# Top-k attention and a Smelu MLP: Smelu from one read of PSUM, the softmax division issued at a step's end, and the first MLP products of a chunk placed among the last ones of the chunk before

## The chip, the core and the metric

The kernel runs on one core of a Trainium2 chip. The metric is device time in microseconds of one execution. TensorE is called PE here, VectorE DVE, ScalarE ACT, GpSimd POOL, and SyncE SP, as the profile calls them.

## What is computed

Top-k attention over 8 batches, 8 heads, 576 positions and head size 64, and behind it an MLP whose activation is Smelu with beta 1:

```python
scores = (1 / np.sqrt(D)) * np.matmul(q, k.transpose(0, 1, 3, 2))
kth = np.partition(scores, -32, axis=-1)[..., -32:-31]
scores = np.where(scores >= kth, scores, -1000000000.0)
attn = np.exp(scores - np.max(scores, axis=-1, keepdims=True))
attn = attn / (np.sum(attn, axis=-1, keepdims=True) + 1e-09)
x = np.matmul(attn, v)                    # then (B, H, S, D) -> (B*S, H*D) = 4608 x 512
h = x @ w_in                              # 512 x 2048
g = np.where(h >= 1, h, np.where(h <= -1, 0.0, (h + 1) ** 2 / 4))
return g @ w_out                          # 2048 x 512
```

The weights of the MLP arrive as float64 and are turned into float32 in the kernel.

## The kernel before

**Steps.** Attention is cut into 144 steps. A step is one tile of 128 queries (or the 64 positions that are left over, two heads at a time) and one pair of heads; DVE does the search for the 32 largest of 576 scores in it (`weights`, lines 271 to 329): four rounds of `max` (L283) and `match_replace` (L292) on the pairwise maxima (L269, L297 makes the pairwise minima), then the masked sum (L312) of the exponentials that ACT wrote (L287), and the reciprocal `rz` (L318). POOL then scales the weights `e` by `rz` (L325; in the early steps PE does it through a diagonal matrix, L322 and L342) and notes a difference in `excess` (L327). `weights` is a generator; each `next` on it issues one part. The last part is the one from `rz` to `excess`.

The rest of a step's attention is on PE and ACT: scores (`scores`, L258, copied out of PSUM by L261), transposes of the weights (`transpose_w`, L344 and L352, copied by L345 and L353), and the product with the values (`values`, L364 and L372, copied into `xT` by L377 and L379). Keys and queries are transposed as they are needed (L214, L222, L238).

**The MLP.** Tiles of 128 tokens are gathered into chunks of one or two tiles (21 chunks; the first four are worked a tile at a time, so with 128 columns, the later ones with two tiles at once, 256 columns). A chunk has 16 units of first products: `hidden` (lines 391 to 415) makes four products into one PSUM tile `ph` (L394) and then Smelu. With `r = relu(h/2 + 1/2)` (L398) and `g = relu(h - 1)` (L412), both read from PSUM by ACT, POOL makes `min(r, 1)` (L413), its square (L414), and adds it to `g` (L415). `r` has 2 buffers, `g` has 16, one for each unit. While weights are still being converted, units with odd `f` square on ACT (L408). The last chunk works on DVE in place of POOL (L403 to L405). For each tile there are 8 units of output products: `final` (L422) makes two 512-column products into the PSUM tile `py`, which has one buffer; behind the last one ACT copies it to `y` (L426) and SP stores it. `ph` and the value product share three PSUM buffers; scores, transposes of the weights, and those of keys and queries share four.

**The order.** All engines but SP run in the program's order, which the planner at the end of `run` writes out (lines 605 to 657). Step `m` begins, when the weights are converted, with the value product of step `m-2` and the scores of step `m+2`; then come seven slots. Slot by slot, `parts` says how many parts of `weights` are issued, slot 2 has the transposes of step `m-1`, slot 4 the transposes of queries and keys, and `advance` issues MLP units from the queue `pending`, as far as the step's `share` lets it. `share` is the smaller of the remaining work over the remaining steps and the pending work over the steps until the next chunk is complete. What is left of `weights` after the slots is issued at the step's end. When a chunk's last value product has been issued, `values_until` appends its units to `pending`: first products, then output products.

```python
parts = [1] * SLOTS if early else [1, 2, 2, 2, 0, 0, 0]
```

With these numbers all seven parts are issued by slot 3, so POOL's queue has L325 and L327 ahead of the Smelu units of slots 3 to 6.

Of the kernel before, what the change touches and what calls it, by code (L numbers as in the profile page):

```python
# [10 lines left out]
F32 = mybir.dt.float32  # L11
U32 = mybir.dt.uint32
I32 = mybir.dt.int32
AF = mybir.ActivationFunctionType
ALU = mybir.AluOpType
# [8 lines left out]
def kernel(  # L24
# [10 lines left out]
    nc = tc.nc  # L35
    B, H, S, D = q.shape
    NTOK, DM = out.shape
    DFF = moe_w_in.shape[1]
    P = 128
# [10 lines left out]
    NF = DFF // P  # L50
# [4 lines left out]
    const = ctx.enter_context(tc.tile_pool(name="const", bufs=1))  # L55
    ident = const.tile([P, P], F32, name="ident")
    make_identity(nc, ident)
    half = const.tile([P, 1], F32, name="half")
    nc.gpsimd.memset(half, 0.5)
    minus = const.tile([P, 1], F32, name="minus")  # L60
    nc.gpsimd.memset(minus, -1.0)
    two = const.tile([P, 1], F32, name="two")
    nc.gpsimd.memset(two, 2.0)

# [17 lines left out]
    n_pieces = NK * DFF // WC + NF * DM // WC  # L82
# [64 lines left out]
    def run(ctx, paired):  # L147
# [240 lines left out]
        def mlp(xT, tiles, pool, last):  # L388
            gs, pys = {}, {}

            def hidden(f, c0, c1):
                ph = ps.tile([P, CW], F32, name="ph", tag="ph", bufs=3)[:, 0:c1 - c0]
                for kk in range(NK):
                    nc.tensor.matmul(ph, w_in[:, kk, f * P:(f + 1) * P], xT[:, kk, c0:c1],  # L394
                                     start=(kk == 0), stop=(kk == NK - 1))

                r = pool.tile([P, CW], F32, name="r", bufs=2)[:, 0:c1 - c0]
                nc.scalar.activation(r, ph, AF.Relu, bias=half, scale=0.5)  # L398
                if f not in gs:
                    gs[f] = pool.tile([P, CW], F32, name="g", bufs=NF)  # L400
                g = gs[f][:, c0:c1]
                if last:
                    nc.vector.tensor_scalar(g, ph, -1.0, 0.0, ALU.add, ALU.max)  # L403
                    nc.scalar.activation(r, r, AF.Square)
                    nc.vector.scalar_tensor_tensor(out=g, in0=r, scalar=1.0, in1=g, op0=ALU.min, op1=ALU.add)  # L405
                    return
                if converted < n_pieces and f % 2:
                    nc.scalar.activation(r, r, AF.Square)  # L408
                    nc.scalar.activation(g, ph, AF.Relu, bias=minus, scale=1.0)
                    nc.gpsimd.tensor_scalar(r, r, 1.0, 0.0, ALU.min, ALU.max)  # L410
                else:
                    nc.scalar.activation(g, ph, AF.Relu, bias=minus, scale=1.0)  # L412
                    nc.gpsimd.tensor_scalar(r, r, 1.0, 0.0, ALU.min, ALU.max)  # L413
                    nc.gpsimd.tensor_tensor(out=r, in0=r, in1=r, op=ALU.mult)  # L414
                nc.gpsimd.tensor_tensor(out=g, in0=r, in1=g, op=ALU.add)  # L415

            def final(i, f0, f1):
                if f0 == 0:
                    pys[i] = ps.tile([P, DM], F32, name="py", tag="py")
                py = pys[i]  # L420
                for f in range(f0, f1):
                    nc.tensor.matmul(py, gs[f][:, i * P:(i + 1) * P], w_out[:, f, :],  # L422
                                     start=(f == 0), stop=(f == NF - 1))
                if f1 == NF:
                    y = pool.tile([P, DM], F32, name="y", bufs=1)
                    nc.scalar.copy(y, py)  # L426
                    for p0, p1, rows in rows_of(*tiles[i]):
                        nc.sync.dma_start(out=rows, in_=y[p0:p1])

            def hiddens(i0, i1):  # L430
                return [(NK * (i1 - i0), NK * (f * P // WC + 1), gs, True, partial(hidden, f, i0 * P, i1 * P))
                        for f in range(NF)]

            def finals(i):
                return [(2 * DM // P, n_pieces - (NF - f - 2) * (DM // WC), gs, False, partial(final, i, f, f + 2))
                        for f in range(0, NF, 2)]

            return gs, hiddens, finals


        rounds, chunks = [], []
# [8 lines left out]
        steps = []  # L450
        for b, t in rounds:
            tile_of = (b, t) if t < NT else (b - b % 2, t)
            ch = next(n for n, tiles in enumerate(chunks) if tile_of in tiles)
# [3 lines left out]
        n = len(steps)  # L457

        EARLY_CHUNKS = 4
# [9 lines left out]
        pending = deque()  # L469
        total, spent = sum(len(tiles) for tiles in chunks) * (NK * NF + NF * DM // P), 0  # L470
        converted, inspected, due = 0, 0, 0.0
# [26 lines left out]
        K_TIME, PIECE_TIME, UNIT_TIME, SLOTS, EARLY_STEPS, EARLY_SHARE = 9.6, 0.55, 0.22, 7, 4, 20  # L498
# [88 lines left out]
        def values_until(m):  # L587
            nonlocal valued, pe_time
            while valued < min(m, n):
                pe_time = max(pe_time, transposed + 1.8) + 1.25  # L590
                values(state[valued])
                state[valued] = None
                if valued in ready:
                    ch, i0, i1 = ready[valued]
                    if i0 == 0:
                        mlps[ch] = mlp(xTs[ch], chunks[ch], mlp_pool, ch == len(chunks) - 1)
                    gs, hiddens, finals = mlps[ch]

                    rest = [work for work in pending if work[2] is gs and not work[3]]
                    while pending and pending[-1][2] is gs and not pending[-1][3]:  # L600
                        pending.pop()
                    pending.extend(hiddens(i0, i1) + rest + [work for i in range(i0, i1) for work in finals(i)])
                valued += 1

        for m in range(n + 2):
            early = converted < n_pieces
            coming = min((r + 2 - m for r in ready if r + 2 > m), default=1)
            if not early:
                values_until(m - 1)
                begin_at(m + 2)  # L610
            share = min((total - spent) / (n + 2 - m), sum(work[0] for work in pending) / coming)
            top_k, parts = None, [0] * SLOTS
            if m < n:
                top_k = weights(state[m], state[m + 1] if m + 1 < n else None)
                parts = [1] * SLOTS if early else [1, 2, 2, 2, 0, 0, 0]
                start = max(dve_time, scored[m])
                now_converting = range(SLOTS) if m < EARLY_STEPS else range(0, SLOTS, 2)
                dve_time = start + K_TIME + PIECE_TIME * min(len(now_converting), n_pieces - converted)
                done[m] = dve_time
                state[m]["by_tensor"] = early  # L620
            for slot in range(SLOTS):
                now = start + (dve_time - start) * (slot + 1) / SLOTS
                for _ in range(parts[slot]):
                    next(top_k, None)
                if m < n and converted < n_pieces:
                    if slot in now_converting:
                        convert(now)
                elif slot == 3:
                    inspect()
                if slot == 1 + (not early) and 1 <= m <= n:  # L630
                    pe_time = max(pe_time, done[m - 1] + 2.0) + 1.0
                    transpose_w(state[m - 1])
                    transposed = pe_time
                if slot == 2 and m == n and paired:
                    judge(ps, att)
                if slot == 2 and early:
                    values_until(m)
                if m == 0 and slot in (1, 2):
                    next(first)
                if slot == 4 and early:  # L640
                    begin_at(m + 2)
                if slot == (5 if early else 4):
                    queries(m + 3)
                    if m < n and prep is None and next_keys < B and steps[m][0] == next_keys - 1 and steps[m][1] >= 1:
                        prep = keys_of(next_keys)
                    if prep is not None and m % 2 == 0:
                        got = next(prep, None)
                        pe_time += 0.5
                        if got is None:
                            prep, next_keys = None, next_keys + 1  # L650
                        else:
                            keys[next_keys] = got
                advance(min(share, EARLY_SHARE if early else share) / SLOTS if m < n else 0.0, now, not early)
            for _ in (top_k if top_k is not None else ()):
                pass
# [50 lines left out]
```

## Time and profile before

| | us |
|---|---|
| median of 3 runs | 1746.18 (1745.42 to 1746.61) |
| the profiled execution | 1746.35 |
| its span, from the first to the last record | 1744.5 |
| PE busy in the span | 1639.4 (94%) |
| DVE busy | 1537.0 (88%) |
| ACT busy | 1083.2 (62%) |
| POOL busy | 946.9 (54%) |
| mean granted clock of PE | 0.982 |

The shares are means over the span. The page's second part shows them in 40 slices, and they differ: in the first tenth PE is busy five to eight tenths and DVE seven to nine; after that PE is at nine tenths or more in each slice but the last, DVE goes between eight and nine until the last two slices, and POOL between one and eight. Records of PE have modelled ends, so that a PE shown as busy may still have gaps.

The page's fourth part, the chain of work that ended last, puts 65% of the span to PE, 14% to DVE, 11% to POOL and 6% to ACT. In the fifth part a group is a line, an engine and a kind of operation, with its count, its busy time and the mean duration of one, and behind the bar the idle time ahead of it and what ended that. The waits are the same idle times summed by who waited for whom. An engine works its queue in order, so whatever stands behind a waiting instruction waits too. A product of float32 matrices is two records on PE.

### The profile page before, as it was taken

How to read it: one execution, taken by the hardware profiler on the slowest of the kernel's cores; microseconds unless marked ns; L12 is line 12 of the kernel's file. 1: busy time of each engine (PE TensorE's matmuls, PEld its weight loads, DVE VectorE, ACT ScalarE, POOL GpSimd, SP SyncE). 2: the span in 40 equal slices, each digit the busy share in tenths (PEclk: the TensorE clock that was granted, in tenths of full speed). 3: DMA queues.
4: the chain of work that ended last, by engine and by line, in shares of the span. 5: the costliest groups of instructions: out<-in, count | busy, mean ns of one | idle time of the engine just before them, and what ended most of it. 6: DMA issues, size and time to landing. Idle time of an engine off the chain costs nothing.

```text
span 1744.5 us, 33535 instructions
## 1 busy us (share of the span) xinstructions
PE 1639.4 (94%) x10665; PEld 1151.5 (66%) x10665; DVE 1537.0 (88%) x4875; ACT 1083.2 (62%) x2942; POOL 946.9 (54%) x1668
## 2 busy tenths in 40 slices
PE   5588989999999999999999999999999999999998
PEld 4476575667766757476756767567667666666665
DVE  7999979888899999999987999999997998899752
ACT  6688575676667857576655647556555555466452
POOL 5689183665544817264646645436365554555550
PEclk7799999999999999999999999999999999999999
DMA  8333112111121112111200101000010000000000
GB/s 253 116 98 97 46 30 65 44 43 41 42 63 52 44 49 65 46 49 41 62 13 22 25 22 44 17 24 17 23 39 19 19 10 14 13 7 7 7 7 15
DMA packets 116668, 74.63 MB, mean 43 GB/s; under 512 B 87296, under 2 KB 95488, under 8 KB 116480
## 3 DMA queue, kind: packets, MB, share of 16 engines
q1 hardware_dynamic: 116480, 72.37, 14.5%
q8 instruction: 87, 1.43, 0.3%
q14 instruction: 101, 0.83, 0.2%
HBM read 62.91 MB, written 9.44 MB: 41 GB/s over the span
## 4 chain that ended last, share of the span: by engine, by line
PE 65%; DVE 14%; POOL 11%; ACT 6%; issue 3%; DMA 0%; POOLq 0%; DVEq 0%; SPq 0%; ACTq 0%
PE py L422 25%; PE ph L394 18%; PE sp L258 7%; PE po L364 7%; PE pw L344 5%; DVE tops L283 4%; DVE more L292 3%; POOL g L415 3%; POOL r L414 3%; DVE e L312 3%; POOL e L325 2%; POOL r L413 2%; ACT s L261 1%; DVE seconds L300 1%; ACT r L398 1%
## 5 line engine op out<-in xcount | busy, mean ns | idle before, releaser
L394 PE MATMUL ph<-xT,w_in 128*128 128x128 f32 (+1 forms) x3200 | 558.0, 326 | 14.4 <-ACT g L412 13.2
L422 PE MATMUL py<-w_out,g 128*128 128x512 f32 x1152 | 530.9, 600 | 2.0 <-ACT y L426 2.0
L394 PEld LDWEIGHTS ph<-xT,w_in 128*128 128x128 f32 x3200 | 472.3, 192 | 87.9 <-ACT g L412 26.0
L325 POOL TENSOR_SCALAR e<-e,rz 128x576 f32<-128x576 f32 x264 | 195.0, 750 | 520.2 <-DVE rz L318 488.8
L283 DVE MAX8 tops<-more 128x8 f32<-128x288 f32 x1152 | 465.4, 445 | 0.0
L292 DVE MATCH_REPLACE8 more<-tops,more 128x288 f32<-128x288 f32 x864 | 375.6, 442 | 0.0
L422 PEld LDWEIGHTS py<-w_out,g 128*128 128x128 f32 x1152 | 205.2, 190 | 224.1 <-issue 215.8
L312 DVE SCALAR_TENSOR_TENSOR e<-s,kth,e 128x576 f32<-128x576 f32 x288 | 245.7, 881 | 116.6 <-ACT e L287 116.3
L398 ACT ACTIVATE r<-ph,half 128x128 f32<-128x128 f32 (+1 forms) x400 | 166.5, 416 | 216.8 <-POOL g L415 156.7
L415 POOL TENSOR_TENSOR g<-r,g 128x128 f32<-128x128 f32 (+1 forms) x384 | 255.9, 666 | 30.2
L413 POOL TENSOR_SCALAR r<-r 128x128 f32<-128x128 f32 (+1 forms) x368 | 173.2, 471 | 132.0 <-ACT r L398 131.7
L414 POOL TENSOR_TENSOR r<-r 128x128 f32<-128x128 f32 (+1 forms) x368 | 213.9, 581 | 30.7
L261 ACT ACTIVATE s<-sp 128x288 f32<-128x288 f32 x576 | 195.2, 421 | 56.8 <-PE sp L258 36.8
L287 ACT ACTIVATE e<-s,nmax 128x576 f32<-128x576 f32 x288 | 213.4, 770 | 7.7
L364 PEld LDWEIGHTS po<-wT,v_in 128*64 128x64 f32 x2048 | 111.8, 137 | 87.9 <-issue 53.2
L258 PE MATMUL sp<-kT,qT 64*128 64x288 f32 x1024 | 163.9, 437 | 4.2 <-ACT kT L218 2.3
L364 PE MATMUL po<-wT,v_in 128*64 128x128 f32 x2048 | 145.5, 280 | 18.7 <-ACT g L412 11.3
L345 ACT COPY wT<-pw 128x512 f32<-128x512 f32 x288 | 154.0, 589 | 13.1 <-PE pw L344 10.6
L344 PEld LDWEIGHTS pw<-ident,e 128*128 128x128 f32 x1056 | 122.2, 142 | 60.0 <-issue 24.4
L344 PE MATMUL pw<-ident,e 128*128 128x128 f32 x1056 | 141.0, 276 | 16.2 <-ACT s L261 10.4
L377 ACT COPY xT<-po 128x128 f32<-128x128 f32 x128 | 34.1, 266 | 195.8 <-PE po L364 195.5
L412 ACT ACTIVATE g<-ph,minus 128x128 f32<-128x128 f32 (+1 forms) x368 | 153.6, 417 | 0.0
(91 smaller groups left out, 1595.1 us busy)
## 6 DMA issues: line engine op xcount, KB each, us to landing
raw<-in_moe_w_out_dram SPq DMA_DIRECT2D x64, 256.0 KB, 2.6
raw<-in_moe_w_in_dram SPq DMA_DIRECT2D x36, 256.0 KB, 2.7
k_in<-in_k_dram SPq DMA_DIRECT2D x64, 128.0 KB, 2.9
q_in<-in_q_dram SPq DMA_DIRECT2D x32, 256.0 KB, 3.1
v_in<-in_v_dram SPq DMA_DIRECT2D x8, 1024.0 KB, 5.8
out_dram<-y SPq DMA_DIRECT2D x32, 256.0 KB, 2.3
kT<-in_moe_w_in_dram SPq DMA_DIRECT2D x16, 256.0 KB, 4.0
v_in<-in_moe_w_in_dram SPq DMA_DIRECT2D x12, 256.0 KB, 4.5
```

The source lines that it names most:

```text
L258: nc.tensor.matmul(o[:, a0 - c0:a1 - c0], qT[d, g, :], kT[d, g, k0:k0 + a1 - a0], start=True, stop=True)
L283: nc.vector.max(out=tops[:, i, r:r + 8], in_=src[:, i, :])
L287: nc.scalar.activation(e[:, i, :], s[:, i, :], AF.Exp, bias=nmax[:, i:i + 1])
L292: nc.vector.match_replace(out=rest[:, i, :], in_to_replace=tops[:, i, r:r + 8], in_values=src[:, i, :], imm_value=LOWEST)
L312: nc.vector.scalar_tensor_tensor(out=e[:, i, :], in0=s[:, i, :], scalar=last[:, i:i + 1], in1=e[:, i, :], op0=ALU.is_ge, op1=ALU.mult, acc ...
L325: nc.gpsimd.tensor_scalar(e[:, i, :], e[:, i, :], rz[:, i:i + 1], 1.0, ALU.mult, ALU.mult)
L344: nc.tensor.transpose(pt[:, c, :], w_in_place, ident)
L364: nc.tensor.matmul(po[j * D:(j + 1) * D], v_in[:, h, c, :] if c < NT else v_tl[0][:, h, :], wT[:, j, c, :] if c < NT else wTt, start=(c == ...
L394: nc.tensor.matmul(ph, w_in[:, kk, f * P:(f + 1) * P], xT[:, kk, c0:c1], start=(kk == 0), stop=(kk == NK - 1))
L414: nc.gpsimd.tensor_tensor(out=r, in0=r, in1=r, op=ALU.mult)
L415: nc.gpsimd.tensor_tensor(out=g, in0=r, in1=g, op=ALU.add)
L422: nc.tensor.matmul(py, gs[f][:, i * P:(i + 1) * P], w_out[:, f, :], start=(f == 0), stop=(f == NF - 1))
```

## The change

Three edits.

- **Smelu.** In the general branch ACT writes `u = relu(h + 1)` into `g`, the only read of PSUM; POOL makes `c = min(u/2, 1)` in `r`, then `g = u - c`, then `g = g * c`. For `u` below 2 that is the square of `u/2`, from there on `u - 1`, which is `h`. The branch of odd units during the conversion and that of the last chunk are as before.
- **Division.** `parts` is `[1, 2, 2, 1, 0, 0, 0]`: the last part of `weights` (the reciprocal, the scaling and `excess`) is issued behind the step's slots.
- **Order of the MLP.** From the fifth chunk on (`EARLY_CHUNKS` is 4), when a new chunk is appended, up to eight of the output units that stand last in `pending` are taken off and put back with the sixteen units of first products between them. `keep` (16 x 512 / 128 = 64 units of cost) is taken off the pending work in `share` when the next chunk is one of those and has two tiles.

```diff
+    one = const.tile([P, 1], F32, name="one")
+    nc.gpsimd.memset(one, 1.0)
...
                 r = pool.tile([P, CW], F32, name="r", bufs=2)[:, 0:c1 - c0]
-                nc.scalar.activation(r, ph, AF.Relu, bias=half, scale=0.5)
                 if f not in gs:
                     gs[f] = pool.tile([P, CW], F32, name="g", bufs=NF)
                 g = gs[f][:, c0:c1]
                 if last:
+                    nc.scalar.activation(r, ph, AF.Relu, bias=half, scale=0.5)
                     nc.vector.tensor_scalar(g, ph, -1.0, 0.0, ALU.add, ALU.max)
                     nc.scalar.activation(r, r, AF.Square)
                     nc.vector.scalar_tensor_tensor(out=g, in0=r, scalar=1.0, in1=g, op0=ALU.min, op1=ALU.add)
-                    return
-                if converted < n_pieces and f % 2:
+                elif converted < n_pieces and f % 2:
+                    nc.scalar.activation(r, ph, AF.Relu, bias=half, scale=0.5)
                     nc.scalar.activation(r, r, AF.Square)
                     nc.scalar.activation(g, ph, AF.Relu, bias=minus, scale=1.0)
                     nc.gpsimd.tensor_scalar(r, r, 1.0, 0.0, ALU.min, ALU.max)
+                    nc.gpsimd.tensor_tensor(out=g, in0=r, in1=g, op=ALU.add)
                 else:
-                    nc.scalar.activation(g, ph, AF.Relu, bias=minus, scale=1.0)
-                    nc.gpsimd.tensor_scalar(r, r, 1.0, 0.0, ALU.min, ALU.max)
-                    nc.gpsimd.tensor_tensor(out=r, in0=r, in1=r, op=ALU.mult)
-                nc.gpsimd.tensor_tensor(out=g, in0=r, in1=g, op=ALU.add)
+                    nc.scalar.activation(g, ph, AF.Relu, bias=one)
+                    nc.gpsimd.tensor_scalar(r, g, 0.5, 1.0, ALU.mult, ALU.min)
+                    nc.gpsimd.tensor_tensor(out=g, in0=g, in1=r, op=ALU.subtract)
+                    nc.gpsimd.tensor_tensor(out=g, in0=g, in1=r, op=ALU.mult)
...
-                    pending.extend(hiddens(i0, i1) + rest + [work for i in range(i0, i1) for work in finals(i)])
+                    new = hiddens(i0, i1)
+                    if i0 == 0 and ch >= EARLY_CHUNKS:
+
+                        places = []
+                        while pending and not pending[-1][3] and len(places) < NF // 2:
+                            places.append(pending.pop())
+                        for x, work in enumerate(reversed(places)):
+                            pending.append(work)
+                            upto = (x + 1) * NF // len(places)
+                            pending.extend(new[x * NF // len(places):upto])
+                        new = [] if places else new
+                    pending.extend(new + rest + [work for i in range(i0, i1) for work in finals(i)])
...
-            share = min((total - spent) / (n + 2 - m), sum(work[0] for work in pending) / coming)
+            next_chunk = steps[m][3] if m < n else 0
+            keep = NF * DM // P if next_chunk >= EARLY_CHUNKS and len(chunks[next_chunk]) == 2 else 0
+            behind = sum(work[0] for work in pending) - keep
+            share = min((total - spent) / (n + 2 - m), max(behind, 0) / coming)
...
-                parts = [1] * SLOTS if early else [1, 2, 2, 2, 0, 0, 0]
+                parts = [1] * SLOTS if early else [1, 2, 2, 1, 0, 0, 0]
```

## The prediction

> **What bounds the kernel now.** I read the page's busy shares, then cut the trace into steps (one step is one call of `weights`: one pair of heads and one query tile, 144 in all), then read the waits and, where a step was long, the timeline.
>
> The page's first part (busy time and share of the span) has two engines nearly full:
>
> ```profile
> PE 1639.4 (94%) x10665; PEld 1151.5 (66%) x10665; DVE 1537.0 (88%) x4875; ACT 1083.2 (62%) x2942; POOL 946.9 (54%) x1668
> ```
>
> The cut uses the start of each step's transposes on TensorE (PE, L342/L344). In the stretches below (the columns are PE, weight load, DVE, ACT and POOL busy time, with instructions) the reader is to see that DVE is full in the second (259 of 268) and has room in the first and last (223 of 266, 306 of 363), while PE has little room anywhere.
>
> ```profile
> 218.10:483.70 265.60, 247.85 (x1864) 182.29 (x1863) 223.15 (x724) 176.28 (x534) 162.41 (x347) 0.99 0.16 45
> 483.70:751.40 267.70, 258.09 (x1667) 175.95 (x1667) 259.16 (x836) 186.35 (x519) 129.68 (x225) 1.00 0.19 54
> 751.40:1095.80 344.40, 337.06 (x2134) 237.37 (x2134) 314.59 (x993) 214.18 (x564) 193.34 (x316) 1.00 0.12 33
> 1095.80:1335.20 239.40, 234.28 (x1405) 156.72 (x1406) 223.14 (x715) 133.22 (x337) 116.17 (x188) 0.99 0.09 24
> 1335.20:1697.80 362.60, 354.42 (x2252) 247.86 (x2251) 306.16 (x964) 201.46 (x524) 207.19 (x366) 1.00 0.04 11
> ```
>
> A busy PE is not a PE at its peak, so I price its work by its fastest rows. In the chain, 32 records of `py` take 13.75, which is 0.86 us for one product (two records); 16 records of `ph` at 256 columns take 3.46, which is 0.43 us for one, and half of that at 128 columns. The rest of a step (8+1 transposes, 10 products with the values, 4 score products) is 3.6: the transposes at 279.9 and 290.3 lie 10.46 apart with eight `py` (6.86) between them. Extra transposes of queries and keys are 0.44 each. DVE's own step is 10.17 without Smelu beside it (reciprocals L318 at 699.30 and 709.48).
>
> Summed over the program's order, PE's own work in the five stretches is 233.6, 251.1, 329.6, 228.3 and 344.9, together 1387.5 of the 1479.7 that they take. So 92 us are lost: 32.0, 16.6, 14.8, 11.1 and 17.7. In the second stretch DVE sets the pace (26 steps x 10.2 is 265). In the others the loss is a stall, and the waits (total us, times, longest) name it:
>
> ```profile
> POOL e L325 <- DVE rz L318: 488.8, 80, 15.0
> ...
> ACT r L398 <- POOL g L415: 156.7, 113, 6.4
> POOL r L413 <- ACT r L398: 131.7, 46, 10.0
> DVE e L312 <- ACT e L287: 116.3, 80, 6.3
> ```
>
> `r` has two buffers. ScalarE (ACT) writes one, GpSimd (POOL) frees it. When POOL stands at the scaling of `e` (L325) for a reciprocal that DVE hasn't made yet, the Smelu behind it stands too, both buffers stay full, and ACT stops at the next L398 with the score copies and the exponentials queued behind it. The timeline shows it once in full (start, duration; idle time before in brackets):
>
> ```profile
> 760.70 1.47 POOL L325 TENSOR_SCALAR e<-e,rz 128x576 f32<-128x576 f32 x2 [5.36 <-DVE rz L318]
> ...
> 763.48 0.72 POOL L415 TENSOR_TENSOR g<-r,g 128x256 f32<-128x256 f32 x1
> ...
> 764.24 0.47 ACT L398 ACTIVATE r<-ph,half 128x256 f32<-128x256 f32 x1 [6.43 <-POOL g L415]
> ...
> 765.11 1.34 ACT L261 ACTIVATE s<-sp 128x288 f32<-128x288 f32 x4
> ...
> 765.69 1.94 PE L344 MATMUL pw<-ident,e 128*128 128x128 f32 x8 [2.89 <-ACT s L261]
> ```
>
> ACT lost 6.43, and PE 2.89 behind it.
>
> **The change, part by part.** *Smelu.* ACT loses one of two activations on 368 of the 400 units (L412: 153.6 us busy), and `r` becomes POOL's alone, so ACT waits no longer for POOL: it writes `g`, which has 16 buffers and is freed by PE products that stand earlier in PE's order. L412 had that same wait, so it isn't new. The cover that goes is POOL's pacing of PE; what is late next is POOL itself, with a backlog that the output products or the scaling meet. POOL keeps three operations, but the square of one operand becomes two operations on two operands:
>
> ```profile
> L415 POOL TENSOR_TENSOR g<-r,g 128x256 f32<-128x256 f32 x176 | 143.8, 817 | 13.8
> ...
> L414 POOL TENSOR_TENSOR r<-r 128x256 f32<-128x256 f32 x176 | 122.8, 697 | 14.7
> ...
> L415 POOL TENSOR_TENSOR g<-r,g 128x128 f32<-128x128 f32 x208 | 112.0, 539 | 16.4
> ...
> L414 POOL TENSOR_TENSOR r<-r 128x128 f32<-128x128 f32 x192 | 91.1, 475 | 16.0
> ```
>
> No row shows a subtraction on POOL. Its bounds are L414 and L415 (0.475 to 0.539 at 128 columns, 0.697 to 0.817 at 256); I take L415, as the nearest in its operands. That adds 0.120 x 176 + 0.064 x 192 = 33 us to POOL, which has over 60 idle in each stretch. (The Trainium skill, "GPSIMD Engine Reference", Elementwise, bounds any two-input operation by one shared read port; by it the square pays as much and the 33 would be 0. The rows differ by 0.06 to 0.12, so I go by them.)
>
> *The scaling at the step's end.* `weights` now issues its last part behind the step's slots, so two L325 and one L327 (1.7 us) move on POOL's queue past the Smelu of slots 3 to 6, up to 4 units. DVE's order is the same: its queue holds nothing else there; SP's is untouched. The transposes that need the scaling stand in the next step's slot 2. Between them PE has 1.24 of values, 1.17 of scores and 3/7 of an MLP share of 6.9, together 5.3. In PE-bound stretches the reciprocal is 8 to 11 us ahead of its transposes, so the scaling must only not fall more than 5.3 behind. The worst place is the first stretch: eight units of 128 columns a step cost POOL 8 x (0.389+0.539+0.539) + 1.7 = 13.4 against PE's 10.5, but for two steps in four or five only. That lag of 3 to 6 us meets the 5.3, so I keep a third of that stretch's stall.
>
> *The new places.* From the fifth chunk on, sixteen first products go two by two among the last eight pairs of output products, and `keep` leaves 64 units of work for it. By the changed order, steps with first products go from 85 to 109 after the 14th, and PE's work in the same five stretches of steps becomes 231.9, 239.1, 331.3, 227.5 and 357.8: the sum is unchanged, but 12.9 us move out of the second stretch, where DVE sets the pace and PE's room is wasted, into the last, where PE sets it. That is a loss of 12 to 13. The copy of `y` (0.59) now has two first products (3.4) instead of sixteen before the next chunk needs the single `py` buffer; with ACT free I cost it at nothing; uncovered, it is 0.6 a chunk, 10 in all.
>
> *Sum.* First stretch: 231.9 + a third of 32 = 242 (-24). Second: DVE, 26 steps x 10.27 = 267 (-1). Third 331.3 + 4 = 335 (-9). Fourth 227.5 + 4 = 231.5 (-8). Last 357.8 + 5 = 363 (0). Before and behind them nothing: the early branch keeps its parts, and the end has the same work. Together -42. The profiled execution is 1746.35 (span 1744.5 and 1.85 around it), the median of the runs shown 1746.18: the forecast is **1704**. With no stall left at all the stretches take 231.9 + 265 + 331.3 + 227.5 + 357.8 = 1413.5, 66 less: 1680. With every stall left, the moved work alone counts: +12, 1758.
>
> **Rivals.** *DVE slows (0.13).* DVE's two-input operations stretch when POOL's Smelu runs beside them: L269 took 0.74 at 707.02 alone and 1.05 at 589.71 beside L415, and DVE's step went from 10.17 to 11.37 (reciprocals at 582.0 and 593.4, four units of 256 columns in it). More steps with Smelu could bring that to all 26 steps of the second stretch: 26 x 11.37 = 296, 29 more than forecast, 1733. Against it: POOL stands before L325 until DVE's step is over, so Smelu of two or three units (2 us each) falls mainly into DVE's searches, which have one input. (The skill's "GPSIMD Engine Reference", Specifications, says the same, that GpSimd contends with two-input Vector instructions; it speaks against spreading and gives no price.)
>
> *The stall changes places (0.11; the slower end).* The scaling, queued behind Smelu, comes so late that PE stands before the transposes as long as it stood before ACT. It decides from the point at which POOL's lag at the end of a step exceeds 5.3, and would hold if that is so in most steps with first products. Then no stall is won and the moved work costs 12, with the 33 on POOL perhaps a few more: 1758 to 1770. Against it: from the fifth chunk a step has at most three or four units (8 us with the scaling) and POOL has 10 to 12.
>
> *All goes (0.14).* No stall stays: 1680.
>
> *No difference (0.04).* Of the 78 us of stalls that lie between 1758 and 1680 only a sixth goes, which just pays the 12 of the moved work: 1746.
>
> **How the numbers follow.** The forecast's case (0.58) spans 1690 to 1720. The range takes in "all goes" with some faster DVE steps, 1674, and the contention case up to 1744; the slower case is left out. Faster by over 0.2% (about what a measurement here tells from no change): 0.58 + 0.14 + 0.13 less a little = 0.84; within: 0.04; slower: 0.12.
>
> **What would show it.** Right: no wait of ACT's Smelu read for POOL; DVE's wait for the exponentials far under 116; the first stretch near 242; POOL's wait for `rz` still long, but with nobody behind it. Wrong: PE's waits before the transposes for L325's successor grow past the 23 us of now; reciprocals in the second stretch 11 apart; the last stretch above 370. The forecast falls if POOL's lag is longer than its rows make it, or if a step's 3.6 on PE hides a wait that I counted as work.

## The result, and the profile after

The changed kernel takes 1859.58 us (median of 4 runs, 1857.64 to 1860.66) against 1745.82 before: a ratio of 1.065 (1.0631 to 1.0668). It is slower, and far outside the range. The profiled execution took 1857.64, its span is 1855.5.

The busy shares and the chain of work that ended last, from the page of the changed kernel:

```profile
PE 1670.8 (90%) x10665; PEld 1168.8 (63%) x10665; DVE 1564.9 (84%) x4875; ACT 997.1 (54%) x2574; POOL 1179.3 (64%) x1669
...
POOL 37%; PE 36%; issue 12%; DVE 11%; ACT 2%; DMA 0%; POOLq 0%; SPq 0%; DVEq 0%; ACTq 0%
```

ACT lost the 368 activations it was meant to lose. POOL is 232 us busier, where 33 were forecast, and its part of the chain went from 11% to 37%. The same five stretches of steps, cut at the transposes as before (PE, weight load, DVE, ACT and POOL busy, then the granted clock of PE):

```profile
220.00:526.90 306.90, 256.46 (x1860) 192.70 (x1858) 227.01 (x732) 160.59 (x445) 197.89 (x350) 0.92 0.14 41
526.90:810.50 283.60, 254.08 (x1635) 174.55 (x1636) 266.97 (x845) 175.03 (x466) 166.77 (x224) 0.98 0.17 48
810.50:1164.60 354.10, 340.69 (x2128) 233.15 (x2126) 320.28 (x983) 192.23 (x486) 247.72 (x308) 1.00 0.12 32
1164.60:1416.20 251.60, 237.74 (x1402) 158.66 (x1403) 228.00 (x709) 122.83 (x296) 152.97 (x188) 0.99 0.09 23
1416.20:1809.60 393.40, 373.76 (x2299) 257.91 (x2297) 309.54 (x964) 178.25 (x434) 271.40 (x373) 0.98 0.04 11
```

| steps | before | forecast | changed kernel |
|---|---|---|---|
| 14 to 36 | 265.6 | 242 | 306.9 |
| 36 to 62 | 267.7 | 267 | 283.6 |
| 62 to 92 | 344.4 | 335 | 354.1 |
| 92 to 113 | 239.4 | 231.5 | 251.6 |
| 113 to 143 | 362.6 | 363 | 393.4 |

Every stretch lost. POOL's groups, kept apart by shape, show where its time came from (count, busy time, mean ns of one):

```profile
L416 POOL TENSOR_SCALAR r<-g 128x256 f32<-128x256 f32 x176 | 202.4, 1150 | 188.1 <-ACT g L415 181.5 <-PE pwt L354 6.3
...
L418 POOL TENSOR_TENSOR g<-g,r 128x256 f32<-128x256 f32 x176 | 146.3, 831 | 13.8
...
L417 POOL TENSOR_TENSOR g<-g,r 128x256 f32<-128x256 f32 x176 | 138.7, 788 | 14.7
L416 POOL TENSOR_SCALAR r<-g 128x128 f32<-128x128 f32 x192 | 135.0, 703 | 150.5 <-ACT g L415 123.7 <-PE pw L346 16.2 <-PE ph L396 10.1
```

L416, `min(u/2, 1)`, takes 1.15 and 0.70 us where L413, `min(r, 1)` with `max 0`, took 0.56 and 0.39. That is 337 us of POOL against 173, most of the 232. And the waits have turned over. After the change (total us, times, longest):

```profile
POOL r L416 <- ACT g L415: 305.2, 105, 16.0
...
DVE e L314 <- ACT e L289: 195.9, 90, 8.9
...
PEld pw L346 <- POOL e L327: 166.7, 117, 6.3
PE pw L346 <- POOL e L327: 117.4, 78, 6.1
```

The same two waits of PE in the kernel before:

```profile
PEld pw L344 <- POOL e L325: 18.8, 22, 2.2
...
PE pw L344 <- POOL e L325: 4.5, 6, 1.2
```

ACT's Smelu read waits for POOL no more. PE now stands before the transposes for POOL's scaling: 166.7 by its weight load, of which 117.4 shows on its products as well, where it was 18.8 and 4.5 (the prediction's 23 is their sum). DVE's wait for the exponentials rose from 116 to 196. One step from the first stretch (start, duration; idle time before in brackets):

```profile
327.73 1.00 POOL L416 TENSOR_SCALAR r<-g 128x128 f32<-128x128 f32 x1 [6.98 <-ACT g L415]
...
329.85 0.17 DVE L320 RECIPROCAL rz<-z 128x2 f32<-128x2 f32 x1
...
344.88 1.47 POOL L327 TENSOR_SCALAR e<-e,rz 128x576 f32<-128x576 f32 x2
345.68 1.12 PE L346 MATMUL pw<-ident,e 128*128 128x128 f32 x4 [6.05 <-POOL e L327]
```

The reciprocal that this scaling needs is there at 330.02. POOL had stood idle for 6.98 us until the step's first unit of Smelu at 327.73, then works off nine units and comes to the scaling only at 344.88, 14.9 us after the reciprocal. PE has done all that stands before the transposes at 339.62 and waits 6.05. It is so in general: with each step's reciprocal, scaling and transposes set side by side, 123.2 of the 123.9 us that PE's products waited before the scaled transposes fall into steps whose scaling began more than 2 us after its reciprocal. Before, those waits were 16.2 in all, and 1.5 of them of this kind.

### The profile page after: what moved, and what is told of

Same layout as the page of the kernel before. It is cut to its first block, busy times and chain, and to the rows that moved or that the text cites. A ratio compares the mean times of both kernels' runs of the same rounds, so it can differ in the third digit from the quotient of the medians.

```text
span 1855.5 us, 32768 instructions
## 1 busy us (share of the span) xinstructions
PE 1670.8 (90%) x10665; PEld 1168.8 (63%) x10665; DVE 1564.9 (84%) x4875; ACT 997.1 (54%) x2574; POOL 1179.3 (64%) x1669
## 4 chain that ended last, share of the span: by engine, by line
POOL 37%; PE 36%; issue 12%; DVE 11%; ACT 2%; DMA 0%; POOLq 0%; SPq 0%; DVEq 0%; ACTq 0%
PE py L425 16%; POOL r L416 12%; POOL g L418 9%; POOL g L417 9%; PE ph L396 8%; POOL e L327 7%; PE sp L260 3%; PE po L366 3%; PE pw L346 3%; DVE tops L285 3%; DVE more L294 2%; DVE e L314 2%; POOL excess L329 1%; DVE seconds L302 1%; ACT e L289 1%
## 5 line engine op out<-in xcount | busy, mean ns | idle before, releaser
L396 PE MATMUL ph<-xT,w_in 128*128 128x128 f32 (+1 forms) x3200 | 569.3, 330 | 0.0
L416 POOL TENSOR_SCALAR r<-g 128x128 f32<-128x128 f32 (+1 forms) x368 | 337.5, 917 | 338.6 <-ACT g L415 305.2
L396 PEld LDWEIGHTS ph<-xT,w_in 128*128 128x128 f32 x3200 | 485.7, 196 | 95.6 <-issue 54.8
L425 PE MATMUL py<-w_out,g 128*128 128x512 f32 x1152 | 542.5, 604 | 2.9 <-ACT y L429 2.9
L314 DVE SCALAR_TENSOR_TENSOR e<-s,kth,e 128x576 f32<-128x576 f32 x288 | 259.7, 930 | 196.8 <-ACT e L289 195.9
L327 POOL TENSOR_SCALAR e<-e,rz 128x576 f32<-128x576 f32 x264 | 221.2, 848 | 194.4 <-DVE rz L320 184.9
L415 ACT ACTIVATE g<-ph,one 128x128 f32<-128x128 f32 (+1 forms) x368 | 152.5, 415 | 276.7 <-PE ph L396 273.4
L346 PE MATMUL pw<-ident,e 128*128 128x128 f32 x1056 | 162.7, 292 | 123.9 <-POOL e L327 117.4
L418 POOL TENSOR_TENSOR g<-g,r 128x128 f32<-128x128 f32 (+1 forms) x368 | 246.6, 670 | 28.8
L417 POOL TENSOR_TENSOR g<-g,r 128x128 f32<-128x128 f32 (+1 forms) x368 | 240.9, 655 | 30.7
L346 PEld LDWEIGHTS pw<-ident,e 128*128 128x128 f32 x1056 | 124.6, 147 | 186.1 <-POOL e L327 166.7
L347 ACT COPY wT<-pw 128x512 f32<-128x512 f32 x288 | 159.7, 585 | 111.3 <-PE pw L346 105.2
L302 DVE MAX8 seconds<-more 128x8 f32<-128x288 f32 x288 | 118.3, 452 | 14.0
```

The costliest lines, as they stand in the source:

```text
L314: nc.vector.scalar_tensor_tensor(out=e[:, i, :], in0=s[:, i, :], scalar=last[:, i:i + 1], in1=e[:, i, :], op0=ALU.is_ge, op1=ALU.mult, acc ...
L327: nc.gpsimd.tensor_scalar(e[:, i, :], e[:, i, :], rz[:, i:i + 1], 1.0, ALU.mult, ALU.mult)
L346: nc.tensor.transpose(pt[:, c, :], w_in_place, ident)
L416: nc.gpsimd.tensor_scalar(r, g, 0.5, 1.0, ALU.mult, ALU.min)
L417: nc.gpsimd.tensor_tensor(out=g, in0=g, in1=r, op=ALU.subtract)
L418: nc.gpsimd.tensor_tensor(out=g, in0=g, in1=r, op=ALU.mult)
```

## The experiments

The line numbers of kernels built on the changed one are two higher than those of before, so L325 is L327 in them. Theory P: the pair of operations in L416 is what is slow, and the scaling is late behind it. Theory D: the scaling at the step's end is late in any case. Theory O: the moved MLP work costs the time, the prediction's one loss. Theory G came up on the way: POOL's rate in runs of first products is the limit. Theory S is the prediction's reading of before: ACT's stops behind the two buffers of `r` are the lost time.

### The pair of operations

```diff
-nc.gpsimd.tensor_scalar(r, g, 0.5, 1.0, ALU.mult, ALU.min)
+nc.gpsimd.tensor_scalar(r, g, 1.0, 0.0, ALU.min, ALU.max)   # a_min_max
+nc.gpsimd.tensor_scalar(r, g, 2.0, 0.5, ALU.min, ALU.mult)  # a_min_mult
```

> The changed kernel with POOL's first Smelu operation as minimum then maximum, min(u, 1) and max 0, in place of multiply then minimum. It leaves out the halving of u, so its output is not the reference's; operands, order and counts are the changed kernel's. Theory P (the pair of operations multiply-minimum is what is slow on POOL: L416 took 0.70 at 128 and 1.15 us at 256 columns where L413 took 0.39 and 0.56): L416 falls to 0.4 to 0.6, the scaling is on time, 1690 to 1720. Theory D (the scaling behind Smelu on POOL is late in any case): 1800 to 1860. Theory O (the moved MLP work costs it): 1800 to 1860. If the slow part is that r is written from g and not in place, L416 stays at 1.1 and the time at 1860.

1772.35 us, ratio to before 1.0153 (1.0136 to 1.0170). L416 fell to 0.54 and 0.40 us. So the pair is worth 87 us in the changed kernel, but the kernel is still 26 slower than before, and neither theory P's 1690 to 1720 nor the forecast's 1704 is reached: theory P is right about the operation and isn't all.

> The changed kernel with min(u, 2) then times 0.5, the same value as min(u/2, 1). If only the pair minimum-maximum is quick, L416 stays near 1.1 us at 256 columns and the time near 1860. If the order of the two operations decides, or a multiply in the second place is quick (the scaling L325, multiply-multiply, takes 1.3 ns an element), L416 falls to 0.4 to 0.6 and the time to 1690 to 1720 by theory P. Theories D and O: 1800 to 1860 either way.

1869.51 us, 1.0714 (1.0696 to 1.0732), L416 at 1.15 and 0.71: the order of the two operations makes no difference to its time.

`b_slow_pair` puts the pair into the kernel before, and nothing else:

```diff
-nc.gpsimd.tensor_scalar(r, r, 1.0, 0.0, ALU.min, ALU.max)
+nc.gpsimd.tensor_scalar(r, r, 1.0, 1.0, ALU.mult, ALU.min)
```

> The kernel before with L413 as multiply by 1 then minimum with 1 (the same value, r is not negative), nothing else. Theory P: L413 goes from 0.39 and 0.56 to about 0.70 and 1.15 us, POOL is some 160 us busier, and with ACT waiting for POOL by the two buffers of r the time goes to 1830 to 1900. Theories D and O say nothing of the pair: 1746 to 1770, with POOL's idle time taking it up.

1847.88 us, 1.0589 (1.0571 to 1.0607). L413 went to 1.16 and 0.72 us, and ACT's wait for POOL from 157 to 308. The pair alone costs 102 us there, in place on `r`, so it isn't that `r` is written from `g`.

`p_pairs` runs POOL alone, each operation four times in a row.

> POOL alone: none of the reference is computed; four of each operation in a row on a tile of 128 partitions at 128, 256 and 512 columns: tensor_scalar with (min, max), (mult, min), (min, mult), (mult, mult), (mult, max), (mult, add), (add, max), min alone, (min, min), and tensor_tensor with mult of one operand by itself, mult, subtract and add of two. Nothing else runs beside them. Theory P: (mult, min) and (min, mult) take 0.63 and 1.06 us at 128 and 256 columns, as L416's shortest do, against 0.29 and 0.40 for (min, max), so some 3.4 ns an element against 0.9. If the durations came from contention with DVE and not from the operation, all pairs are alike here, 0.3 to 0.4.

From its groups at 256 and 128 columns (L43 is min and max, L45 mult and min, L49 mult and mult, L57 min alone; L65 subtracts two tensors):

```profile
L45 POOL TENSOR_SCALAR y<-x 128x256 f32<-128x256 f32 x4 | 4.3, 1068 | 0.3
...
L57 POOL TENSOR_SCALAR y<-x 128x256 f32<-128x256 f32 x4 | 3.4, 845 | 0.3
...
L65 POOL TENSOR_TENSOR y<-x,y 128x256 f32<-128x256 f32 x4 | 2.9, 722 | 0.3
...
L45 POOL TENSOR_SCALAR y<-x 128x128 f32<-128x128 f32 x4 | 2.6, 642 | 0.3
...
L49 POOL TENSOR_SCALAR y<-x 128x256 f32<-128x256 f32 x4 | 1.6, 404 | 0.3
L43 POOL TENSOR_SCALAR y<-x 128x256 f32<-128x256 f32 x4 | 1.6, 400 | 0.3
...
L43 POOL TENSOR_SCALAR y<-x 128x128 f32<-128x128 f32 x4 | 1.2, 293 | 2.5 <-DMA x<-in_q_dram 2.3
```

Multiply-minimum costs 3.3 ns an element ((1068 - 642) / 128), minimum-maximum 0.8. The pairs are of two kinds: min-max, mult-mult and mult-add took 0.40 us at 256 columns; mult-min, min-mult, mult-max, add-max and min-min all took 1.06 to 1.07, more than a subtraction of two tensors. A minimum alone took 0.85, so a second operation can make it quicker. No DVE work ran beside them, so this isn't contention. What POOL does differently for them stays open.

### The three parts, each taken back

`a_old_smelu` is the changed kernel with the Smelu of before; `b_division` is before with the division alone:

```diff
-parts = [1] * SLOTS if early else [1, 2, 2, 2, 0, 0, 0]
+parts = [1] * SLOTS if early else [1, 2, 2, 1, 0, 0, 0]
```

> The changed division and order of MLP work with the Smelu of before. Theory P: no slow pair, but ACT waits for POOL again: 1735 to 1775, the moved work (12 us) and the stalls of before. Theory D: the scaling is late at the step's end, 1800 to 1850. Theory O: 1800 to 1850.

1757.48 us, 1.0071 (1.0054 to 1.0088): within theory P's range; theories D and O had 1800 and more.

> The kernel before with the division alone moved to the step's end. Theory D: the scaling comes late in steps with many units, PE stands before the transposes: 1760 to 1785. If the prediction's cover of 5.3 us holds: 1715 to 1746, since ACT's waits for POOL behind a scaling that has no reciprocal yet go away.

1773.56 us, 1.0162 (1.0145 to 1.0179): the division alone loses 28 us on the kernel before, within theory D's 1760 to 1785, and the prediction's cover doesn't hold.

With the quick pair (halving left out), `m_old_division`, `m_old_order` and `m_smelu_only` take back the division, the order (no units between the others and `keep = 0`), or both.

> The changed kernel with the quick pair (minimum, maximum; the halving of u is left out, so the output isn't the reference's) and with the division back in slot 3. With the quick pair alone the time was 1772, 26 over before, and its first stretch (14th to 36th step) 279 where the prediction had 242. Theory D (what is left of the loss is the scaling behind Smelu at the step's end): the first stretch falls to 240 to 255, the whole to 1705 to 1735. Theory O (what is left is the moved MLP work): 1760 to 1775, the last stretch stays at 370. Theory G (POOL's own rate in the steps with 128-column units sets the pace wherever the scaling stands): first stretch 265 to 280, the whole 1750 to 1770.

1720.53 us, 0.9856 (0.9840 to 0.9873); the first stretch fell from 279.3 to 248.1, as theory D had it.

> The changed kernel with the quick pair (halving left out) and with the order of MLP work of before; the division stays at the step's end. Theory O: the last stretch falls from 371 to about 358, the whole to 1745 to 1755. Theory D: the first stretch stays at 279, the whole at 1760 to 1790, since without the spreading more units stand ahead of each scaling. Theory G: as D.

1803.27 us, 1.0330 (1.0312 to 1.0347): theory O, which had 1745 to 1755, is out, and it is 13 over theory D's range.

> The Smelu of the change with the quick pair (halving left out) on the kernel before, division and order untouched. If ACT's waits for POOL were what the kernel before lost (the prediction's first step), its stretches fall to PE's own work plus a few us: 1680 to 1715. Theory G: POOL's rate holds it, 1735 to 1750.

1719.53 us, 0.9851 (0.9835 to 0.9868). That is 4.5 over the range for ACT's waits as the loss, and 15 under theory G's 1735 to 1750. The first stretch took 248.2; the prediction's terms for it with the order of before, 233.6 and a third of 32, make 244.

The same step in two of them shows what the division's place does. In `m_smelu_only` the scaling stands behind four of the step's nine units, by POOL's timeline, and by PE's it meets the transposes without a wait:

```profile
317.30 1.47 POOL L327 TENSOR_SCALAR e<-e,rz 128x576 f32<-128x576 f32 x2
```

```profile
322.89 1.04 PE L346 MATMUL pw<-ident,e 128*128 128x128 f32 x8
```

In `m_old_order`, the same Smelu and order with the division at the step's end, all nine stand ahead of it. The reciprocal is there at 320.05, and POOL begins the scaling only at 332.40, so that PE's transposes wait:

```profile
317.69 0.66 POOL L416 TENSOR_SCALAR r<-g 128x128 f32<-128x128 f32 x1 [6.98 <-ACT g L415]
...
319.88 0.17 DVE L320 RECIPROCAL rz<-z 128x2 f32<-128x2 f32 x1
...
327.53 2.05 PE L396 MATMUL ph<-xT,w_in 128*128 128x128 f32 x16
...
332.40 1.47 POOL L327 TENSOR_SCALAR e<-e,rz 128x576 f32<-128x576 f32 x2
...
333.20 1.97 PE L346 MATMUL pw<-ident,e 128*128 128x128 f32 x8 [3.62 <-POOL e L327]
```

PE stood still from 329.6 to 333.2, and the transposes took 1.97 in place of 1.04, which is the clock (below). The wait is handed on: ACT's copies of the transposes (L347) wait for PE 82 us here and 22 in `m_smelu_only`, what stands behind them in ACT's queue comes later, and DVE's masked sum waits 136 us for the exponentials, against 62. That is not what made the scaling late in this step, whose reciprocal lay ready for 12.35 us; whether it costs time of its own is not shown.

`m_div_slot5` issues the division in slot 5:

```diff
-parts = [1] * SLOTS if early else [1, 2, 2, 2, 0, 0, 0]
+parts = [1] * SLOTS if early else [1, 2, 2, 1, 0, 1, 0]
```

> The kernel of 1719.5 (quick pair with the halving left out, order of before) with the division issued in slot 5 in place of slot 3; at the step's end the same kernel took 1803. Theory D (each unit of Smelu put in front of the scaling delays the transposes by POOL's lag): between the two, 1745 to 1785. If only a place behind the whole step's units costs anything: 1720 to 1735.

1754.71 us, 1.0050 (1.0032 to 1.0067). Slot 3, slot 5 and the end give 1719.5, 1754.7 and 1803.3: the more Smelu is put in front of the scaling, the longer it takes, as theory D has it.

### POOL's rate and the order

`f_smelu_only` and `f_old_division` make the same `c` with two quick operations, on the order of before and on the changed one, both with the division in slot 3:

```diff
-nc.gpsimd.tensor_scalar(r, g, 0.5, 1.0, ALU.mult, ALU.min)
+nc.gpsimd.tensor_scalar(r, g, 2.0, 0.0, ALU.min, ALU.max)
+nc.gpsimd.tensor_scalar(r, r, 0.5, 1.0, ALU.mult, ALU.mult)
```

> The Smelu of the change on the kernel before, division and order untouched, with c made by two quick operations, min(u, 2) with max 0 and then times 0.5 times 1: the same value as the change's. POOL has four operations a unit, 0.3 (128 columns) to 0.4 us (256) more than with the one quick operation that left the halving out (1719.5). Theory G (POOL's rate beside ACT's freedom): 1725 to 1745. If POOL's rate is covered once the scaling isn't behind it: 1718 to 1725.

1833.64 us, 1.0500 (1.0482 to 1.0517). This I missed by 89: one more quick operation, 0.47 and 0.36 us a unit, costs 114 us.

> The changed kernel with c from two quick operations (the same value) and the division back in slot 3. Without the changed order the same Smelu took 1833.6. Theory G: POOL has 0.36 to 0.47 us a unit more than the one quick operation (1720.5) and less than or about as much as the slow pair (1760.1), and spread units keep it under the limit: 1735 to 1760. If the order is worth nothing, as the pair 1720.5 and 1719.5 says for a quick POOL: about 1830.

1769.07 us, 1.0135 (1.0118 to 1.0152), 9 over theory G's range, and far from the 1830 of an order worth nothing. `a_old_division`, `a_smelu_only` and `a_old_order` do the same for the Smelu of the change with its slow pair.

> The changed kernel, slow pair and all, with the division back in slot 3. With the quick pair that put 1772 to 1720. Theory P alone (the pair costs its 88 us wherever the scaling stands): 1805 to 1815. If the pair costs only by making the scaling late, the time falls further: 1730 to 1770.

1760.08 us, 1.0077 (1.0060 to 1.0094). Against the quick pair's 1720.5 the pair still costs 40 here, so being late with the scaling is much of its price and not all.

> The change's Smelu alone, slow pair and all, on the division and order of before. Theory G (a POOL at its limit in runs of first products): POOL has 0.34 to 0.59 us a unit more than with the one quick operation, about as much as the four quick ones (1833.6) or a little more: 1830 to 1870. If the slow pair's 88 us of the changed kernel add up: 1805.

1836.10 us, 1.0511 (1.0494 to 1.0529), within theory G's range.

> The changed kernel with the order of MLP work of before (slow pair, division at the step's end). Theory G with D: slow POOL, unspread units and the scaling behind all of them, the worst of all, 1900 to 1960. If the three parts only add: 1860 and the order's 31 us, 1890.

1984.51 us, 1.1360 (1.1341 to 1.1379), more than any theory had. All twelve places of the table (medians, us):

| Smelu | slot 3, order of before | slot 3, changed order | step's end, order of before | step's end, changed order |
|---|---|---|---|---|
| of before | 1745.8 | 1738.6 | 1773.6 | 1757.5 |
| one read, quick pair (halving left out) | 1719.5 | 1720.5 | 1803.3 | 1772.4 |
| one read, the change's pair | 1836.1 | 1760.1 | 1984.5 | 1859.6 |

The parts don't add. In the change's row the division costs 148 in the old order and 99.5 in the new one, and the order is worth 76 and 125. A sum for a step of the later chunks suggests why. With four units of 256 columns PE needs 4 x 1.72 + 3.6 = 10.5. POOL needs four times its three means and 1.7 for the scaling: 4 x (0.54 + 0.82 + 0.80) + 1.7 = 10.3 with the quick pair, 4 x (1.15 + 0.79 + 0.83) + 1.7 = 12.8 with the change's, and about 12.4 with two quick operations (0.52 + 0.47 + 0.85 + 0.83). The quick one is just under PE's step, the others above it, and in the old order such steps follow each other. The changed order has two or three units in most steps. That sum agrees with which of the six kernels with the division in slot 3 gain from the order, not with how much; it was not tested by itself, and it does not speak of the first stretch. There, where both orders are alike, the quick pair took 248, the change's 279 and 281, two quick operations 283 in either order, so that some 31 to 35 us of the loss stand outside it.

`b_order` has the changed order alone.

> The kernel before with the MLP order of the change alone (two reads of PSUM by ACT, division in slot 3). Theory O, the prediction's price for the moved work: 1755 to 1762. Theory G (spreading the first products takes load from POOL where it is the limit, which is worth more than the moved work): 1715 to 1740; with the quick one-read Smelu the order changed nothing (1720.5 against 1719.5).

1738.62 us, 0.9957 (0.9941 to 0.9974): a gain of 6.5, where the prediction had a loss of 12. The last stretch does lose, but 3.3 (365.9 against 362.6). The third gains 9 (335.3 against 344.4), and that is more. Theory G's range holds.

### The buffers of r

`b_r5` gives `r` five buffers, by letting odd units use a tile that is free after the conversion:

```diff
-r = pool.tile([P, CW], F32, name="r", bufs=2)[:, 0:c1 - c0]
+more_room = converted >= n_pieces and f % 2
+r = pool.tile([P, CW], F32, name="units" if more_room else "r", bufs=3 if more_room else 2)[:, 0:c1 - c0]
```

> The kernel before with five buffers for r in place of two (units with odd f take the three of the tile units, which is free once the weights are converted); no operation and no order is changed. Theory S (the prediction's reading of before: ACT's stops behind r's two buffers are the lost time): ACT is as free as with one read of PSUM, and POOL has its old operations, so 1700 to 1725, about as the quick one-read Smelu (1719.5). Theory G (POOL's rate is the limit and ACT's stops only show it): 1735 to 1750.

1707.26 us, 0.9780 (0.9764 to 0.9797), within theory S's range and the fastest kernel of all here. Its waits:

```profile
POOL e L325 <- DVE rz L318: 456.3, 77, 15.0
...
DVE e L312 <- ACT e L287: 70.9, 61, 6.3
```

POOL waits for reciprocals nearly as long as before (456, it was 489). ACT's stop for POOL's `g` is 20, it was 157. The five stretches took 246.2, 266.6, 336.4, 235.8 and 354.7; the forecast's terms, less the moved work, make 244 for the first.

> Five buffers for r and the changed MLP order on the kernel before, division in slot 3, Smelu's operations as before. If buffers and order are worth their time apart and add: 1690 to 1715. If both only relieve the same stall: no better than the better of the two.

1714.67 us, 0.9821 (0.9805 to 0.9838). It is no better than the better of the two. With ACT free and POOL at its old rate the changed order costs 7.4: the last stretch loses 10.7 (365.4 against 354.7), near the 12 that the prediction had, and the others give some of it back.

## Why the prediction was wrong

- **What bounds the kernel before: right in the mechanism, too large by some 40%.** Taking away only the shortage of buffers gave 38 us, so the stall that the prediction read from the waits is there to be won; its gain for the stretches, without the moved work, was some 54. The change's own way to it, the one-read Smelu with POOL as quick as priced, gave 25 (`m_smelu_only`).
- **The Smelu's price on POOL: the step that failed first.** "eight units of 128 columns a step cost POOL 8 x (0.389+0.539+0.539)": 0.389 is L413's, minimum with maximum, set down for multiply with minimum without a word that the operations differ. It measured 0.703 (1.150 at 256 columns against 0.560). No row of before shows that pair, so it was an unseen price and had to be bounded like the subtraction. Its cost in the changed kernel is 87 us. The two-tensor operations, to which the prediction gave its care, came out as priced: 0.53 and 0.52, 0.79 and 0.83.
- **The scaling's cover of 5.3 us: failed.** "That lag of 3 to 6 us meets the 5.3, so I keep a third of that stretch's stall." With POOL as quick as the prediction had it, the first stretch took 281 with the division at the end and 248 with it in slot 3, and the whole lost 84 us in the old order (1803.3 against 1719.5) and 52 in the new. The sum set POOL's work of a whole step against PE's whole step, as if POOL could begin when PE does. In the step of `m_old_order` shown, PE begins at 313.05 and POOL's first unit comes only at 317.69; nine units, not eight, then take 14.7 us (1.63 each, where the sum had 1.47). So POOL reaches the scaling 7.3 us after PE's step has ended (325.12), and PE's cover there is 4.5, not 5.3. In the same step of the changed kernel the lag is 9.7. Over all steps of `m_old_order`, 67 of the 77.5 us that PE's products waited before these transposes fall into steps whose scaling began over 2 us after its reciprocal.
- **The second rival had the mechanism**, "the stall changes places", at 0.11 and with 1758 to 1770. Its condition, a lag of over 5.3 at a step's end, is what the traces show, and the changed kernel with the quick pair gave 1772. What took it to 1860 is the first failed step, which that rival did not have either.
- **The moved work: right in size where nothing else binds** (7 us with five buffers, 11 in the last stretch; by the prediction's own figures 12.0 leave the second stretch and 12.9 enter the last). Elsewhere it was outweighed: that spreading first products relieves POOL, which the prediction did not count at all, fits the table and was not tested by itself.
- **DVE's contention: not seen as a cause.** With the quick pair and the division in slot 3 the second stretch took 266.8 in the changed order and 271.0 in the old one, at 267.7 before. In the changed kernel the reciprocals of that stretch are indeed 11.4 apart on average (10.6 before), but DVE is only 8 us busier in it (267.0 against 259.2).
- **The copy of `y`: as forecast**, PE's weight load waited 6.5 for it in all, 4.5 before.
- **PE's clock: not in the prediction.** See below; it may make part of the larger losses.

Laid out along one path: Smelu alone +90, the order on top of it -76, the division on top of both +99.5; together the 114.

## What to carry to other kernels

A fused operation is priced by its own pair of operations: a row with the same shape and engine but another pair says nothing of it, and is to be bounded or measured alone first. When an instruction is moved behind others on a queue, its cover must be set against the backlog of that queue at its worst, counted from when the queue can begin on it. And where an engine stops because a neighbour holds its buffers, try more buffers before rewriting the arithmetic.

## What the runs showed of the hardware

POOL's multiply-minimum at four times the price per element of minimum-maximum was not expected.

Nor was the clock's part. After the wait of the changed kernel shown above, the granted clock (the third column from the right) went down and came back:

```profile
340.00:345.00 5.00, 0.00 (x0) 0.00 (x0) 4.84 (x19) 0.63 (x2) 4.60 (x9) 0.73 0.01 2
345.00:348.00 3.00, 2.32 (x11) 2.32 (x12) 2.97 (x9) 0.90 (x2) 2.84 (x6) 0.50 0.00 0
...
350.00:352.00 2.00, 2.00 (x19) 1.76 (x19) 0.34 (x1) 1.99 (x7) 1.84 (x4) 1.00 0.02 7
```

PE had no product in the first of these, and the four transposes behind it took 1.12, where eight took 1.04 in `m_smelu_only`. Over the whole span the mean granted clock was 0.966 against 0.982 before: 1855.5 x 0.034 = 63 us of clock not granted against 1744.5 x 0.018 = 31, so at most some 32 of the 114 us may be that: part of it falls into PE's own waits, as in the first of these windows, and costs nothing. In the slowest kernel, `a_old_order`, it was 0.940, in `b_r5` 0.985. The Trainium skill, "TensorE: Matmul & The Clock Gate", Why this matters for your kernels, advises against gaps of over about 3 us between bursts of products, as the clock then falls to half; here the waits of 3.6 us (`m_old_order`, 0.50 from 334 to 338) and 6.05 us were followed by half the clock, which agrees.
